# Attention and feed-forward on one core: two queues for the first q and k, gain products on GpSimd, w_in in one go, sums of the last heads in pieces

## The chip, the cores and the metric

The kernel runs on 1 core of one Trainium2 chip. The time is device microseconds of one launch. The kernel before took 425.52 us, the median of three runs (425.33 to 425.61). Inside the core five engines work from instruction queues of their own and meet at semaphores: TensorE (PE, whose weight loads stand apart as PEld), VectorE (DVE), ScalarE (ACT), GpSimd (POOL) and SyncE (SP). SP, ACT and POOL can issue DMAs. In the profile, queue q1 is what SP issues, q0 is what POOL issues, and q10 is what ACT issues.

## The reference, cut to what matters

Eight batches of twelve heads with 448 positions and 64 values a head. Rows of q and k are normalised to unit root mean square and multiplied by gains; attention follows, and its result goes through a feed-forward layer of 768 to 2048 to 768 with a tanh GELU.

```python
def rmsnorm(x, g):
    rms = np.sqrt(np.mean(x * x, axis=-1, keepdims=True) + 1e-06)
    return x / rms * g
q_n, k_n = (rmsnorm(q, g_q), rmsnorm(k, g_k))
scores = np.matmul(q_n, k_n.transpose(0, 1, 3, 2)) / np.sqrt(64)
scores = scores - np.max(scores, axis=-1, keepdims=True)
attn = np.exp(scores)
attn = attn / (np.sum(attn, axis=-1, keepdims=True) + 1e-09)
x = np.matmul(attn, v)            # -> (tokens, 768), heads side by side
h = x @ w_in
g = 0.5 * h * (1.0 + np.tanh(c * (h + 0.044715 * h * h * h)))
out = g @ w_out
```

## The kernel before

**Tiles.** A batch b has three chunks c of four heads. A chunk's q or k is one tile `raw` of 128 x 2 x 7 x 64 floats: two heads by 64 rows on the partitions, two pairs of heads a, and seven tiles t of positions. `square` squares it, `total` sums the squares on DVE (L139), `rsqrt` makes the inverse root on ACT with a logarithm and an exponential (L163 to L173), `normed` multiplies (L210), `turn` transposes on PE (L228) and `put` copies from PSUM to `qT` or, with the product of the two gains as a factor, to `kT` (L237 to L241). The gains come by two small DMAs to `grow`; `gprod` is their product, `gcols` its transpose, `gdiag` a diagonal matrix of it, and the matmul `gall` with `gdiag` yields the bound `shift` that the exponential takes in place of the row's maximum.

**Units.** `unit(b, c, t)` has four score matmuls `sc` (L270) and one exponential `ex` of 128 x 896 on ACT (L274). There are two score buffers in PSUM, so the scores of a unit wait for the exponential two units earlier. `products(b, c, 0)` adds the exponentials up over the keys with a matrix of ones, 28 matmuls; `products(b, c, 1)` multiplies them with v, 28 more (both L315). Both write the PSUM pair `oall`, so the second has to wait until `turned` (two 32 x 32 transposes on DVE, L324) has read the sums. `recips` makes reciprocals in every row (L330, L331), `quad_x` multiplies and writes `xT` (L339).

**Order.** The order is written out by hand. `first_attention` walks the 21 units of batch 0 and calls, after unit i, the functions that the table `mid` holds for slot i, and before it those of `side` (loads of batch 1). `idle(n, warm())` issues n matmuls of zeros that only keep PE busy. After the last unit come the sums and products of chunk 2 and the first two pairs of the first feed-forward matmul (`mm1_pair`, L412: two columns of 128 of w_in, "early" for the inputs of chunks 0 and 1, "late" for those of chunk 2, then the GELU at L417). Six more pairs follow, beside them the norms of batch 1, whose middle chunk is transposed by DMA (`dma_trans`, L251). Then `attention(1, ...)` runs the units of batch 1 two at a time with the second feed-forward matmul of batch 0 between them (`mm2`, L368): 96 matmuls, first all that use the left half of w_out, from the 49th on those that use the right half (`order.sort`, L429).

**Queues.** SP issues q and k of every chunk and the transposes, in program order. POOL issues the gains, v, w_in as two halves of four DMAs each (`w_in_part`, L544) and w_out as two halves (`w_out_part`, L547), all in its own order of work, between squares and norms. A tile of raw q or k has four buffers, so the load of a chunk waits for the norm of the chunk four before it; one buffer (`held`) is kept back until `released`.

**The front before** is these lines: ACT squares the halves of q, then of k, and each norm's root is made as soon as its two sums are there; DVE makes the gain products between the sums of k.

```python
    for n, ns in (("q", q_only), ("k", k_only)):
        for a in range(2):
            square(0, 0, n, nc.scalar, slice(a, a + 1))
            ...
            total(0, 0, n, slice(a, a + 1))
        rsqrt(0, 0, ns, (1,) if n == "k" else ())
    normed(0, 0, "q", nc.gpsimd)
    square(0, 1, "q", nc.gpsimd)
    square(0, 1, "k", nc.gpsimd)
    load_v(0, 0, HP)
```

Of the kernel before, what the change touches and what calls it, by code (L numbers as in the profile page):

```python
# [17 lines left out]
def kernel(  # L18
# [50 lines left out]
    zeros = consts.tile([128, S], BF16)  # L69
    nc.vector.memset(zeros, 0.0)  # L70
# [4 lines left out]
    for i, row in enumerate((g_q, g_k)):  # L75
        nc.gpsimd.dma_start(
            grow[:, i].rearrange("(j p) d -> j p d", j=2)[:, 0],
            row.rearrange("(j d) -> j d", j=2),
        )
# [20 lines left out]
    def load(b, c, n, parts=1, eng=nc.sync):  # L100
        t = rawqk.tile([P, 2, NT, D], F32, tag=f"raw{n}", name=f"raw{n}")
        src = {"q": q, "k": k}[n]
        raws[n, b, c] = t
        m = 2 // parts
        return [
            lambda i=i: eng.dma_start(
                t[:, i * m:(i + 1) * m].rearrange("p a t d -> p a (t d)"),
                src[b, 4 * c + 2 * i * m:4 * c + 2 * (i + 1) * m].rearrange(
                    "(a r) (p t) d -> (r p) a (t d)", r=2, t=NT
                ),  # L110
            )
            for i in range(parts)
        ]
# [86 lines left out]
    def idle(n, w):  # L200

        for _ in range(n):
            nc.tensor.matmul(w, zeros[:, :128], zeros, start=True, stop=True)
# [94 lines left out]
    def products(b, c, what, part=0, parts=1):  # L298

        if part == 0:  # L300
            oas[what] = [o[:, :S] for o in oall]
            if b == 0 and c + 1 == NCH and not what:
                oas[what] = [
                    ps_m.tile([128, 512], F32, tag="mm", name="os")[:, :S] for r in range(2)
                ]
        o = oas[what]
        es = [exs[b, c][:, t] for t in range(NT)]
        if not what and added(b, c):
            es[:added(b, c) + 1] = [ess[b, c]]
        n = len(es)  # L310
        for i in range(n * part // parts, n * (part + 1) // parts):
            for r in range(2):
                rs = slice(r * R, (r + 1) * R)
                for a in range(2):
                    nc.tensor.matmul(  # L315
                        o[r][a * D:(a + 1) * D],
                        vb[b % 2][rs, 2 * c + a, i] if what else ones[rs], es[i][rs, a],
                        start=(i == 0), stop=(i == n - 1),
                    )
# [168 lines left out]
    def first_attention(side, mid):  # L488

        for i in range(NCH * NT):  # L490
            for fn in side.get(i, ()):
                fn()
            unit(0, i // NT, i % NT)
            for fn in mid.get(i, ()):
                fn()
        nc.scalar.preload_act_table_set(GELU_SET)
        square(1, 2, "q", nc.scalar)
        square(1, 2, "k", nc.scalar)
        c = NCH - 1
        products(0, c, 0, 1, 2)  # L500
        turned()
        products(0, c, 1)
        recips()
        mm1_pair(0, early)
        quad_x(0, c)
        mm1_pair(1, early)
        mm1_pair(0, late)
        mm1_pair(1, late)
# [7 lines left out]
    for n in "qk":  # L516
        for go in load(0, 0, n, 2):
            go()
# [48 lines left out]
    for n, ns in (("q", q_only), ("k", k_only)):  # L567
        for a in range(2):
            square(0, 0, n, nc.scalar, slice(a, a + 1))
            if (n, a) == ("k", 1):  # L570
                for h in range(2):
                    nc.vector.tensor_mul(gprod[h * D:(h + 1) * D], grow[:, 0], grow[:, 1])
                nc.vector.transpose(gcols, gprod)
                nc.vector.tensor_scalar(gdiag, ident[:D, :D], gcol[:D], None, op0=ALU.mult)
            total(0, 0, n, slice(a, a + 1))
        rsqrt(0, 0, ns, (1,) if n == "k" else ())
    normed(0, 0, "q", nc.gpsimd)
# [5 lines left out]
    w_in_part(0, 2)  # L583
    gall = ps_s.tile([128, 2, 512], F32, tag="sc", name="gall")[:, 0, :D]
    nc.tensor.matmul(gall, rows, gdiag, start=True, stop=True)
    idle(3, warm())
    turn(0, 0, "q")
    put(0, 0, "q", eng=nc.scalar)
    normed(0, 0, "k", nc.vector, t_first)
    turn(0, 0, "k", t_first)  # L590
# [3 lines left out]
    nc.vector.tensor_scalar(shift, shift, 60.0, 0.0, op0=ALU.add, op1=ALU.min)  # L594
    put(0, 0, "k", t_first)
    idle(3, warm())
# [3 lines left out]
    def released():  # L600
        for t in held:
# [17 lines left out]
            lambda: products(0, 0, 0, 0, 2)),  # L619
           (8, lambda: products(0, 0, 0, 1, 2), lambda: turned(), lambda: recips(),  # L620
            lambda: rsqrt(0, 2, near=(1,)), lambda: normed(0, 2, "q", nc.gpsimd),
            lambda: normed(0, 2, "k", nc.vector, t_first),
            lambda: w_in_part(1, 2),
# [5 lines left out]
           (10, lambda: products(0, 0, 1, 0, 2)),  # L629
           (11, lambda: products(0, 0, 1, 1, 2)),  # L630
# [3 lines left out]
           (15, lambda: products(0, 1, 0, 0, 2), lambda: total(1, 0, "q"),  # L634
            lambda: total(1, 0, "k")),
           (16, lambda: products(0, 1, 0, 1, 2), lambda: turned(), lambda: recips()),
           (18, lambda: products(0, 1, 1, 0, 2)),
           (19, lambda: products(0, 1, 1, 1, 2), lambda: quad_x(0, 1)),
           (20, lambda: products(0, 2, 0, 0, 2))]
# [107 lines left out]
```

## Time and profile before

| | |
|---|---|
| median of three runs | 425.52 us (425.33 to 425.61) |
| the profiled execution's own time | 423.37 us |
| its span | 421.6 us, so 1.77 us lie outside the span |
| PE busy | 405.7 us (96%) |
| ACT busy | 274.9 us (65%) |
| DVE busy | 259.8 us (62%) |
| POOL busy | 124.3 us (29%) |
| first scores / first exponential / last exponential of batch 0 ends | 11.10 / 11.54 / 35.48 us |
| first matmul of the feed-forward layer | 37.28 us |
| first scores of batch 1 | 57.58 us |

All times below are from the start of the span. A line of the timeline gives start, duration, engine, line, operation, out<-in, how many, and in brackets how long the engine had been idle and what ended that. The chain that ended last is followed back from the last instruction, each step to what released it. A row of the windows holds the busy time of PE, PEld, DVE, ACT and POOL in that stretch, each with the number of instructions in brackets, then the granted PE clock as a share, the mean busy share of the DMA engines, and GB/s. A queue's row in the DMA view holds packets, MB and the share of the DMA engines.

### The profile page before, as it was taken

How to read it: one execution, taken by the hardware profiler on the slowest of the kernel's cores; microseconds unless marked ns; L12 is line 12 of the kernel's file. 1: busy time of each engine (PE TensorE's matmuls, PEld its weight loads, DVE VectorE, ACT ScalarE, POOL GpSimd, SP SyncE). 2: the span in 40 equal slices, each digit the busy share in tenths (PEclk: the TensorE clock that was granted, in tenths of full speed). 3: DMA queues.
4: the chain of work that ended last, by engine and by line, in shares of the span. 5: the costliest groups of instructions: out<-in, count | busy, mean ns of one | idle time of the engine just before them, and what ended most of it. 6: DMA issues, size and time to landing. Idle time of an engine off the chain costs nothing.

```text
span 421.6 us, 8029 instructions
## 1 busy us (share of the span) xinstructions
PE 405.7 (96%) x3321; PEld 205.7 (49%) x3321; DVE 259.8 (62%) x430; ACT 274.9 (65%) x364; POOL 124.3 (29%) x98
## 2 busy tenths in 40 slices
PE   5879999999999999999999999999999999999995
PEld 2336554545444544455444554445445454445563
DVE  4887947945689357973689455992589504891010
ACT  5885468838876587838877478747878348754300
POOL 5793515292202640063301840054400900000000
PEclk9998999999999999999999999999999999999999
DMA  7999999589521946249511958239411621130033
GB/s 261 208 256 243 218 192 280 96 205 264 78 62 41 241 79 181 76 104 294 98 39 39 215 129 191 64 83 268 64 46 39 125 45 38 39 75 3 0 75 76
DMA packets 65316, 54.06 MB, mean 128 GB/s; under 512 B 37376, under 2 KB 60288, under 8 KB 65280
## 3 DMA queue, kind: packets, MB, share of 16 engines
q1 hardware_dynamic: 52992, 41.66, 38.0%
q0 software_dynamic: 12128, 11.80, 17.7%
q8 instruction: 26, 0.43, 0.4%
q10 hardware_dynamic: 160, 0.10, 0.1%
q14 instruction: 10, 0.08, 0.1%
HBM read 45.61 MB, written 11.01 MB: 134 GB/s over the span
## 4 chain that ended last, share of the span: by engine, by line
PE 86%; ACT 9%; DVE 2%; POOL 2%; issue 1%; DMA 1%; DVEq 0%; ACTq 0%; POOLq 0%
PE o L368 32%; PE h L348 23%; PE hh L412 12%; PE o L315 9%; PE sc L270 8%; ACT ex L274 5%; ACT L710 2%; DVE ss L139 1%; POOL sq L134 1%; PE tp L228 1%; ACT g L354 1%; DMA rawq<-in_q_dram 1%; POOL win L544 1%; PE os L315 0%; DVE nrmk L210 0%
## 5 line engine op out<-in xcount | busy, mean ns | idle before, releaser
L274 ACT ACTIVATE ex<-sc,shift 128x896 bf16<-128x896 f32 x168 | 159.2, 1004 | 33.3 <-PE sc L270 31.9
L368 PE MATMUL o<-wout,g 128*128 128x384 bf16 x896 | 159.3, 327 | 0.0
L368 PEld LDWEIGHTS <-g 128*128 128x128 bf16 x896 | 81.3, 98 | 71.3 <-issue 23.3
L348 PE MATMUL h<-xT,win 128*128 128x448 bf16 x504 | 96.5, 352 | 0.0
L139 DVE TENSOR_REDUCE ss<-sq 128x14 f32<-128x896 f32 (+1 forms) x43 | 44.4, 1039 | 55.6 <-ACT sq L132 51.6
L348 PEld LDWEIGHTS <-win 128*128 128x128 bf16 x504 | 49.3, 98 | 46.0
L354 ACT ACTIVATE g<-h 128x448 bf16<-128x448 f32 x84 | 45.6, 543 | 28.2 <-PE h L348 23.1
L391 DVE COPY osb<-o 128x384 f32<-128x384 f32 x51 | 28.0, 550 | 58.3 <-PE o L368 58.0
L270 PE MATMUL sc<-qT,kT 64*64 64x448 bf16 x672 | 53.7, 366 | 4.7 <-ACT ex L274 3.5
L417 ACT ACTIVATE g<-hh 128x896 bf16<-128x896 f32 x22 | 19.3, 915 | 57.1 <-PE hh L412 57.1
L412 PE MATMUL hh<-xT,win 128*128 128x448 bf16 x264 | 52.9, 353 | 0.3 <-ACT g L417 0.3
L557 POOL COPY mark<-es 1x1 bf16<-1x1 bf16 x6 | 1.1, 177 | 139.7 <-DVE es L292 139.7
L210 POOL TENSOR_TENSOR nrmq<-rawq,rinv 128x896 bf16<-128x896 f32 x21 | 35.5, 1689 | 17.8 <-DVE o L195 11.9
L315 PE MATMUL o<-ex,vb 64*64 64x448 bf16 x672 | 38.1, 357 | 1.4 <-DVE st L324 1.4
L412 PEld LDWEIGHTS <-win 128*128 128x128 bf16 x264 | 24.6, 98 | 26.1 <-issue 5.0
L270 PEld LDWEIGHTS <-kT 64*64 64x64 bf16 x672 | 17.5, 104 | 37.1 <-issue 33.8
L210 POOL TENSOR_TENSOR nrmk<-rawk,rinv 128x896 bf16<-128x896 f32 x19 | 31.9, 1679 | 0.0
L324 DVE STREAM_TRANSPOSE st<-o 128x448 f32<-128x448 f32 x46 | 27.0, 625 | 6.8 <-PE o L315 6.7
L339 DVE TENSOR_TENSOR xT<-o,rb 128x448 bf16<-128x448 f32 x48 | 27.6, 618 | 4.7 <-PE o L315 4.2
L134 POOL TENSOR_TENSOR sq<-rawq 128x896 f32<-128x896 f32 x9 | 15.6, 1733 | 50.5 <-DVE ss L139 37.8
L315 PEld LDWEIGHTS <-vb 64*64 64x64 bf16 x672 | 20.4, 108 | 15.1 <-issue 4.6
L295 DVE TENSOR_TENSOR e<-ex 128x896 bf16<-128x896 bf16 x38 | 23.2, 611 | 7.0 <-ACT ex L274 7.0
(77 smaller groups left out, 266.0 us busy)
## 6 DMA issues: line engine op xcount, KB each, us to landing
out_dram<-osb SPq DMA_DIRECT2D x54, 192.0 KB, 2.7
rawq<-in_q_dram SPq DMA_DIRECT2D x23, 448.0 KB, 4.4
rawk<-in_k_dram SPq DMA_DIRECT2D x23, 448.0 KB, 4.9
vb<-in_v_dram POOLq DMA_DIRECT2D x8, 672.0 KB, 6.7
win<-in_moe_w_in_dram POOLq DMA_DIRECT2D x8, 384.0 KB, 13.7
wout<-in_moe_w_out_dram POOLq DMA_DIRECT2D x2, 1536.0 KB, 29.4
rawq<-in_q_dram SPq DMA_DIRECT2D x2, 224.0 KB, 2.6
rawk<-in_k_dram SPq DMA_DIRECT2D x2, 224.0 KB, 4.2
```

The lines of the kernel that those rows point to most:

```text
L139: nc.vector.reduce_sum(sss[b][:, c, "qk".index(n), hs], sqs[n, b, c][:, hs], axis=AX.X)
L210: eng.tensor_mul(nrms[n, b, c][:, ts].rearrange("p t a d -> p a t d"), raws[n, b, c][:, :, ts], root[:, :, ts].to_broadcast([P, 2, m, D]),)
L270: nc.tensor.matmul(sc[r * R:(r + 1) * R, a, :S], kT[rs, c, t, r], qT[b][rs, c, :, r], start=True, stop=True,)
L274: nc.scalar.activation(ex[:, t], sc[:, :, :S], AF.Exp, scale=scale, bias=shift)
L315: nc.tensor.matmul(o[r][a * D:(a + 1) * D], vb[b % 2][rs, 2 * c + a, i] if what else ones[rs], es[i][rs, a], start=(i == 0), stop=(i == n ...
L324: nc.vector.transpose(st[:, r].rearrange("p a b -> p (a b)"), oas[0][r])
L339: nc.vector.tensor_mul(xT[b][:, 2 * c + r], oall[r][:, :S], oas["rb"][:, r])
L348: nc.tensor.matmul(h[:, :S], win[:, c, f * 128:(f + 1) * 128], xT[b][:, c], start=(c == 0), stop=(c == HP - 1),)
L354: nc.scalar.activation(g[:, f, (b % 2) * S:(b % 2 + 1) * S], h[:, :S], AF.Gelu_apprx_tanh)
L368: nc.tensor.matmul(o[:, :HD], g[:, f, i * 128:(i + 1) * 128], wout[:, f, half * HD:(half + 1) * HD], start=(f == 0), stop=(f == nf - 1),)
L391: nc.vector.tensor_copy(part, o[:, :HD])
L412: nc.tensor.matmul(h[:, j, :S], win[:, c, f * 128:(f + 1) * 128], xT[b][:, c], start=(c == 0), stop=(c == HP - 1),)
```

## The change

Six things change, all of them in what is issued before the end of batch 0's attention.

The first q and k still come as two halves each, but the first half of both is issued by SP and the second half of both by ACT. ACT issues the second half of q, the two gains and the second half of k, in this order, and only then loads its table of exponentials; before, SP issued all four halves and POOL the gains. The clearing of `grow` comes ahead of that of `zeros`.

The two products of the gains and the scaling of the identity move from DVE to GpSimd; their transpose stays on DVE and stands between the sums of q and those of k.

The root of q is made after the squares of k, not ahead of them, with that of k behind it. GpSimd norms q in two parts, four tiles and three tiles of positions; PE turns and ACT copies them in these parts too, with the first part of k turned between them. The bound `shift` is made ahead of k's norm, and one warming matmul fewer is issued.

The second half of w_in is issued right behind the first, ahead of the norm of q of chunk 2. Before it was issued behind that norm.

The sums of squares of batch 1's first chunk are taken later by DVE: q's at slot 14, k's at slot 16 and behind `turned` and `recips` of chunk 1; before, both came ahead of them.

The sums of chunk 2 get their own PSUM pair (`spared`) at slot 17 and are made in pieces: three of the seven key tiles at slot 17, three behind the products of chunk 1 at slot 20, one after the last unit. Before, three were made at slot 20 and four after the last unit. The products of chunk 1 are cut in three pieces over slots 18, 19 and 20 where they were two, at 18 and 19.

```diff
-    zeros = consts.tile([128, S], BF16)
-    nc.vector.memset(zeros, 0.0)
...
-    for i, row in enumerate((g_q, g_k)):
-        nc.gpsimd.dma_start(
+    zeros = consts.tile([128, S], BF16)
+    nc.vector.memset(zeros, 0.0)
+    def load_gains():
+        for i, row in enumerate((g_q, g_k)):
+            nc.scalar.dma_start(
...
-    def products(b, c, what, part=0, parts=1):
-        if part == 0:
-            oas[what] = [o[:, :S] for o in oall]
-            if b == 0 and c + 1 == NCH and not what:
-                oas[what] = [
-                    ps_m.tile([128, 512], F32, tag="mm", name="os")[:, :S] for r in range(2)
-                ]
+    spare = []
+    def spared():
+        spare.append(
+            [ps_m.tile([128, 512], F32, tag="mm", name="os")[:, :S] for r in range(2)]
+        )
+    def products(b, c, what, lo=0, hi=NT):
+        if lo == 0:
+            oas[what] = spare.pop() if spare else [o[:, :S] for o in oall]
...
-        for i in range(n * part // parts, n * (part + 1) // parts):
+        for i in range(lo, min(hi, n)):
...
-        products(0, c, 0, 1, 2)
+        products(0, c, 0, 6)
...
-    for n in "qk":
-        for go in load(0, 0, n, 2):
-            go()
+    halves = [go for pair in zip(load(0, 0, "q", 2, (nc.sync, nc.scalar)),
+                                 load(0, 0, "k", 2, (nc.sync, nc.scalar))) for go in pair]
+    halves[0]()
+    halves[2]()
+    load_gains()
+    halves[1]()
+    halves[3]()
     nc.scalar.preload_act_table_set(EXP_SET)
...
     idle(16, warm())
-    for n, ns in (("q", q_only), ("k", k_only)):
+    for h in range(2):
+        nc.gpsimd.tensor_mul(gprod[h * D:(h + 1) * D], grow[:, 0], grow[:, 1])
+    for n in "qk":
         for a in range(2):
             square(0, 0, n, nc.scalar, slice(a, a + 1))
-            if (n, a) == ("k", 1):
-                for h in range(2):
-                    nc.vector.tensor_mul(gprod[h * D:(h + 1) * D], grow[:, 0], grow[:, 1])
-                nc.vector.transpose(gcols, gprod)
-                nc.vector.tensor_scalar(gdiag, ident[:D, :D], gcol[:D], None, op0=ALU.mult)
             total(0, 0, n, slice(a, a + 1))
-        rsqrt(0, 0, ns, (1,) if n == "k" else ())
-    normed(0, 0, "q", nc.gpsimd)
+        if n == "q":
+            nc.vector.transpose(gcols, gprod)
+    nc.gpsimd.tensor_scalar(gdiag, ident[:D, :D], gcol[:D], None, op0=ALU.mult)
+    rsqrt(0, 0, q_only)
+    rsqrt(0, 0, k_only, (1,))
+    normed(0, 0, "q", nc.gpsimd, t_first)
+    normed(0, 0, "q", nc.gpsimd, t_rest)
     square(0, 1, "q", nc.gpsimd)
     square(0, 1, "k", nc.gpsimd)
     load_v(0, 0, HP)
     square(0, 2, "q", nc.gpsimd)
     square(0, 2, "k", nc.gpsimd)
     w_in_part(0, 2)
+    w_in_part(1, 2)
...
-    turn(0, 0, "q")
-    put(0, 0, "q", eng=nc.scalar)
-    normed(0, 0, "k", nc.vector, t_first)
-    turn(0, 0, "k", t_first)
+    turn(0, 0, "q", t_first)
+    put(0, 0, "q", t_first, nc.scalar)
     nc.vector.tensor_reduce(
         shift, gall, axis=AX.X, op=ALU.max, apply_absolute_value=True, negate=True
     )
     nc.vector.tensor_scalar(shift, shift, 60.0, 0.0, op0=ALU.add, op1=ALU.min)
+    normed(0, 0, "k", nc.vector, t_first)
+    turn(0, 0, "k", t_first)
+    turn(0, 0, "q", t_rest)
+    put(0, 0, "q", t_rest, nc.scalar)
     put(0, 0, "k", t_first)
-    idle(3, warm())
+    idle(2, warm())
...
              lambda: normed(0, 2, "k", nc.vector, t_first),
-            lambda: w_in_part(1, 2),
             lambda: square(1, 0, "q", nc.gpsimd), lambda: square(1, 0, "k", nc.gpsimd),
...
-           (15, lambda: products(0, 1, 0, 0, 2), lambda: total(1, 0, "q"),
+           (14, lambda: total(1, 0, "q")),
+           (15, lambda: products(0, 1, 0, 0, 3)),
+           (16, lambda: products(0, 1, 0, 3), lambda: turned(), lambda: recips(),
             lambda: total(1, 0, "k")),
-           (16, lambda: products(0, 1, 0, 1, 2), lambda: turned(), lambda: recips()),
+           (17, lambda: spared(), lambda: products(0, 2, 0, 0, 3)),
            (18, lambda: products(0, 1, 1, 0, 2)),
-           (19, lambda: products(0, 1, 1, 1, 2), lambda: quad_x(0, 1)),
-           (20, lambda: products(0, 2, 0, 0, 2))]
+           (19, lambda: products(0, 1, 1, 2, 4)),
+           (20, lambda: products(0, 1, 1, 4), lambda: quad_x(0, 1),
+            lambda: products(0, 2, 0, 3, 6))]
```

## The prediction

> **What bounds the kernel now.** I read the page first (PE busy 96%), then the chain that ended last for the first 75 us, the timeline of the same stretch, the clock by windows, and the DMA queues stretch by stretch.
>
> The front, by the timeline:
>
> ```profile
> 3.31 1.11 ACT L132 ACTIVATE sq<-rawq 128x448 f32<-128x448 f32 x2 [1.28 <-DMA rawq<-in_q_dram]
> 5.75 1.68 POOL L210 TENSOR_TENSOR nrmq<-rawq,rinv 128x896 bf16<-128x896 f32 x1 [2.96 <-ACT rinv L173]
> 6.79 0.58 ACT L132 ACTIVATE sq<-rawk 128x448 f32<-128x448 f32 x1 [0.66 <-DMA rawk<-in_k_dram]
> 8.38 1.68 POOL L134 TENSOR_TENSOR g<-rawq 128x896 f32<-128x896 f32 x1 [0.95 <-DMA rawq<-in_q_dram]
> 11.10 0.38 PE L270 MATMUL sc<-qT,kT 64*64 64x448 bf16 x4
> ```
>
> k's second half lands at 6.79 and sets the first scores at 11.10. The middle, by the chain:
>
> ```profile
> 22.99 2.53 POOL win L544 x4
> 25.54 3.34 POOL sq L134 x2
> 28.90 1.08 DVE ss L139
> 29.98 1.10 DVE st L324 x2
> ```
>
> GpSimd issues half of w_in, so its squares are late, DVE waits for them, and PE for DVE's transposes. ACT then idles 1.94 us at 32.60 and 0.86 us at 34.47. By windows, the stretch with the stall is followed by one at half clock:
>
> ```profile
> 28.03:31.44 3.41, 1.50 (x26) 0.63 (x21) 2.82 (x5) 2.64 (x3) 3.41 (x4) 1.00 1.11 263
> 31.44:34.85 3.41, 3.41 (x44) 2.25 (x39) 2.22 (x3) 1.39 (x2) 3.41 (x3) 0.50 1.11 249
> ```
>
> So far the change aims well. The next place is decisive. The chain around 69 us, the timeline there and later, and the DMA view from 34 us on:
>
> ```profile
> 68.35 1.41 PE o L368 x8
> 69.75 0.04 issue
> 69.79 0.32 PE o L368
> ```
>
> ```profile
> 68.28 1.84 PE L368 MATMUL o<-wout,g 128*128 128x384 bf16 x9
> 78.30 1.64 PE L368 MATMUL o<-wout,g 128*128 128x384 bf16 x9
> ```
>
> ```profile
> wout<-in_moe_w_out_dram POOLq DMA_DIRECT2D x1, 1536.0 KB, 35.6
> ```
>
> The right half of w_out is issued at 34.12 and lands 35.6 us later, at 69.75; the first matmul that reads it (the 49th, last of those nine) starts at 69.79. Nine such matmuls take 1.64 us elsewhere and 1.84 here: PE waits 0.2 us already. What comes earlier than this place gains nothing unless this landing comes earlier. The queues, for 45 to 53, 53 to 63 and 63 to 70 us:
>
> ```profile
> q0 software_dynamic: 2046, 1.64, 129.8%
> q1 hardware_dynamic: 1, 0.00, 0.0%
> ```
>
> ```profile
> q0 software_dynamic: 1860, 1.43, 90.9%
> q1 hardware_dynamic: 1836, 0.47, 36.6%
> ```
>
> ```profile
> q1 hardware_dynamic: 1255, 2.08, 93.0%
> q0 software_dynamic: 200, 0.15, 14.2%
> ```
>
> q0 (w_out, v) runs alone, 0.205 MB/us, then beside SP's transposes at 0.143, and only its last 0.15 MB meet the raw q and k of batch 2.
>
> **The change part by part.**
>
> *Two queues, and roots later.* ACT issues four DMAs: 0.41 us each by SP's rows, 0.60 by ACT's own at the end (two in 1.20). Its table load (1.28) then ends at 3.9 to 4.4 instead of 2.03, say 4.2; four squares of 0.56 make 6.45. When k's second half lands is not shown: at best 5.5 (the four halves' 0.92 MB have passed by 5.3, by the windows' GB/s, and the first landing lagged its bytes by 0.65, less what the gains cost), at worst 6.79 as now. q's root (0.31 + 0.22) thus comes at 7.0 to 7.95, against 5.67. I take 7.2: the bytes bind more than the issue. GpSimd's first part is 4/7 of 1.68, 0.96; the second 0.72. The first scores then come at 9.8 to 10.65, 1.3 to 0.45 us earlier. SP's loads for chunk 1 are issued 0.9 us earlier (two issues fewer) and meet k's second half, which is why I don't take 5.5. One warming matmul fewer (0.2) and the order of two clears cost nothing: PE waits there. Gain products on GpSimd have no row; 0.1 (its memsets) to 0.57 us each (DVE's) fit into the 2.96 us that it idles before 5.75, and they take 1.0 us (0.77 + 0.23) off DVE. If the gains landed late, DVE's transpose would hold k's sums; before, the second landed 4.6 us after its issue at 2.22, but behind 0.56 to 0.74 us of GpSimd issue.
>
> *GpSimd behind it.* Its first square moves from 8.38 to 8.7 or 9.65, and with it the sum for chunk 1 and the root at 14.22: of the front's gain 1.0 to 0.0 us is left. The second half of w_in (2.53 us) goes into the 2.95 us that GpSimd idled from 18.41; it ends at 20.94 plus 0.3 to 1.3, and q's norm of chunk 2 behind it started at 21.35. So chunk 2's scores come 0.5 us earlier at best and 0.4 later at worst; I take 0.4 earlier. w_in itself lands no sooner: q0 is never empty, in the same order.
>
> *The stall.* GpSimd's squares for batch 1 come 2.5 us earlier, and DVE's two sums (1.08 each) stand behind what PE waits for: DVE's waits of 0.55 twice go, PE's 1.29 and 0.15 too, and ACT's 1.94 and 0.86. Twelve of the sixteen last sums (57 ns each, 0.7 us) move ahead of the last exponential; their cover is PE's wait for DVE at slot 17, and if it is gone they cost 0.7 there. Exponentials back to back (0.92) from 25.17 end at 32.5 instead of 35.48. DVE has the products of chunk 1 to scale first (1.16), so the feed-forward starts at 34.45 instead of 37.35: 2.9 us. With the front, batch 0's attention is 3.3 us shorter (2.5 to 3.4).
>
> *What is late next.* The second half of w_in lands at 42.9 and is needed by the fifth pair, at 46.9 less 3.3: 43.6, just in time (batch 2's first loads, issued 2.4 us earlier behind GpSimd's release, can hold it up by up to 1 us). The right half of w_out is not: PE is there at 66.3 and stands until it lands. And it lands later. The transposes of batch 1 wait for GpSimd's norms (47.37), these for DVE's roots, and these for the end of chunk 2, so SP issues them 3.3 us earlier, and the raw loads of batch 2 behind them. q0 loses 3.3 us of running alone and has 3.3 x 0.205 = 0.68 MB more left when the raw loads begin (59.7 instead of 63). Beside raw loads it moved 0.38 MB in the 4 us from 39 to 43, 0.095 MB/us. So 0.68 MB take 7.1 us, to 66.8, and the 0.15 MB of before, which took 6.75 us, end at 73.5. That is the upper bound; SP's last raw load lands at 73.95 and then q0 would be alone. The lower bound spreads all 0.83 MB evenly over the engines: 59.7 + 8.7 = 68.4. I take 72.0, nearer the upper, because the uneven tail is in the trace. PE resumes 2.2 us later than before.
>
> The DMA view of those 4 us, where both queues had work:
>
> ```profile
> q0 software_dynamic: 419, 0.38, 57.4%
> q1 hardware_dynamic: 419, 0.72, 55.9%
> ```
>
> As many packets of the one as of the other. By the Trainium skill (DMA: Bandwidth & Descriptors, "Queues, rings and completion order") an engine alternates between the queues that have work, packet by packet. The trace agrees, and by this rule the sum is the one above. If instead q0's older work were served first, the landing would stay at 69.75; that is the first rival below.
>
> *The clock.* A stretch of 3.41 us with PE busy 1.50 was followed by 3.41 us at 0.50, which cost 1.7 us of PE work; a standstill of 3 to 7 us does the same, and PE works without a pause behind it. Between 0 and 2.4 us are lost, by where the stretch falls; I take 1.2. The Trainium skill (TensorE: Matmul & The Clock Gate, "Part 1: The HAM clock gate") states a free-running window of 3413 ns; the trace's two stretches fit, and by it the loss is the same but its phase is not the kernel's to choose.
>
> *Sum.* 2.2 + 1.2 = 3.4 us slower: 426.8 for the profiled execution's 423.37. That one ran 2.15 us under the median of the runs; against the median, 425.5 + 3.4 = 428.9. The ends: 1.4 faster with no clock loss, 424.1; 3.7 + 1.7 slower, 430.9. Least of all this depends on the front.
>
> **The rivals.**
>
> *The landing stays at 69.75* because q0's work is served first. The gain is waited away, the clock costs 0 to 1.7: 425.3 to 427.2. The packets of 39 to 43 us speak against it. Chance 0.18, half of it within 0.2%.
>
> *Faster: the uneven tail of q0 goes away.* Without the 6.75 us in which a few engines finish 0.15 MB, w_out lands early. For 0.2% it has to land by 68.9 and PE to keep its clock; landing at 66.4 gives the whole 3.4, 422.1. For it: the first v landed without such a tail, so something between 18 and 24 us makes it, and the order there changes. Likeliest time 423.3. Chance 0.20.
>
> *The front fails.* k's second half lands at 6.79, GpSimd is 1.3 us late, w_in's second half holds up chunk 2 by 0.4. The attention is 2.5 us shorter, q0 starts later by up to 1.3 us, the landing is at 71.2 to 72.5: 427.5 to 429. Chance 0.12.
>
> *My forecast* has 0.50, and 427 to 430.9 as its own range. Slower by over 0.2% (0.85 us, about what measurement can tell from no change): 0.50 + 0.12 + 0.09 = 0.71; within: 0.09; faster: 0.20. The range reaches into the faster case, to 423.8, and to 431.
>
> **What would show it.** Right: the feed-forward starts near 34.0; the first transpose by DMA is issued near 45.8; the 49th matmul of L368 ends an idle time of PE of over 3 us, released by w_out's landing after 70.5; a window at 0.50 behind it and none around 32. For the front: q's table load on ACT ends near 4.2, k's squares begin before 6.8, first scores by 10.2. Wrong: w_out landing before 69, or PE not waiting there; or a start of the feed-forward later than 36, which would leave too little shift for the rest to follow.

## The result, and the profile after

The changed kernel takes 431.63 us (median; 427.60 to 432.22). Its ratio to the kernel before is 1.0132, 95% interval 1.0095 to 1.0170: slower by 1.3%. The forecast was 428.9 with a range of 423.8 to 431.0, so the direction held and the size did not: the medians differ by 6.1 us where 3.4 was forecast. The profiled execution took 431.12 us with a span of 429.3 us, 7.7 us more than before.

The timeline of the front of the changed kernel (start, duration, engine; the lines answer to those of before, with new line numbers):

```profile
1.22 1.08 ACTq L78 DMA_DIRECT2D grow<-in_g_q_dram  x1
2.33 0.50 ACTq L78 DMA_DIRECT2D grow<-in_g_k_dram  x1
2.86 0.41 ACTq L109 DMA_DIRECT2D rawk<-in_k_dram  x1
8.87 0.58 ACT L135 ACTIVATE sq<-rawk 128x448 f32<-128x448 f32 x1 [2.77 <-DMA rawk<-in_k_dram]
10.03 1.83 POOL L213 TENSOR_TENSOR nrmq<-rawq,rinv 128x512 bf16<-128x512 f32 x2 [2.67 <-DMA rawk<-in_k_dram]
11.82 1.68 POOL L137 TENSOR_TENSOR g<-rawq 128x896 f32<-128x896 f32 x1
13.35 0.59 PE L273 MATMUL sc<-qT,kT 64*64 64x448 bf16 x4
15.08 1.04 POOL L125 DMA_DIRECT2D vb<-in_v_dram  x1
```

The second half of k, issued by ACT behind the gains, lands at 8.85 where it landed at 6.77. GpSimd starts the norm of q at 10.03 instead of 5.75, the first scores come at 13.35 instead of 11.10, and v, the first load in q0, is issued at 15.08 instead of 11.64. The front has lost 2.25 us at the scores and 3.44 us at q0. The wait of 2.67 us before the norm stands against a DMA of k, but it ends with q's root: the root is ready at 9.89, and in the same front with w_out in rows, further below, the norm starts at 10.04 behind the root (ACT rinv).

The chain of the changed kernel around the feed-forward layer:

```profile
35.31 40.26 DMA wout<-in_moe_w_out_dram
75.58 0.04 issue
75.62 0.48 PE o L374
```

The right half of w_out is issued 1.2 us later than before, takes 40.26 us instead of 35.6, and is now 9% of the chain. What PE lost to it stands in the page's group of the second feed-forward matmuls (busy us and mean ns, then idle time and what ended most of it; before, that idle time was 0.0):

```profile
L374 PE MATMUL o<-wout,g 128*128 128x384 bf16 x896 | 159.7, 328 | 4.9 <-DMA wout<-in_moe_w_out_dram 4.9
```

PE resumes at 75.62 instead of 69.79, 5.83 us later. The rest, about 1.9 us, lies in the clock, by the windows of the changed kernel:

```profile
8.33:11.74 3.41, 0.61 (x8) 0.45 (x8) 1.59 (x4) 1.66 (x6) 1.71 (x2) 1.00 0.46 177
11.74:18.57 6.83, 6.46 (x33) 1.91 (x32) 3.44 (x5) 4.33 (x8) 6.81 (x6) 0.50 0.66 156
69.77:73.18 3.41, 0.95 (x6) 0.47 (x5) 3.34 (x6) 0.46 (x1) 2.52 (x3) 1.00 1.12 337
73.18:80.01 6.83, 4.39 (x39) 1.58 (x38) 0.66 (x2) 1.91 (x2) 1.67 (x1) 0.50 0.95 218
```

Twice a stretch with an idle PE is followed by 6.83 us at half clock: once in the front, where PE waits for q and k, and once behind the wait for w_out, where PE was busy 4.39 us at half clock and so got about 2.2 us less done. The first scores of batch 2 come at 113.85 instead of 105.98, 7.9 us later, and nothing is lost from there on.

The granted clock of a whole execution differs from run to run of one kernel (0.983 in three runs of the changed kernel, which took 431.12 to 432.22 us, and 0.992 in the one of 427.60), so a profiled execution can lie several us from its kernel's median. Ratios below leave out the slow runs, those more than 1.5% above the fastest of their kernel: one of the eight of the front alone (431.88 us) and two of the six of one queue with w_out in rows (427.11 and 427.80; with them the means give 0.996 there, with an interval that reaches past 1). Medians are of all runs, and the other numbers are those of one profiled execution.

### The profile page after: what moved, and what is told of

It is laid out like the page before. It is cut to its first block, busy times and chain, and to the rows that moved or that the text cites. A ratio compares the mean times of both kernels' runs of the same rounds, so it can differ in the third digit from the quotient of the medians.

```text
span 429.3 us, 8029 instructions
## 1 busy us (share of the span) xinstructions
PE 409.4 (95%) x3320; PEld 205.1 (48%) x3320; DVE 258.7 (60%) x427; ACT 275.0 (64%) x365; POOL 124.1 (29%) x100
## 4 chain that ended last, share of the span: by engine, by line
PE 76%; DMA 11%; POOL 5%; ACT 5%; issue 1%; SPq 0%; DVE 0%; ACTq 0%; POOLq 0%
PE o L374 30%; PE h L354 22%; DMA wout<-in_moe_w_out_dram 9%; PE o L321 8%; PE hh L418 8%; PE sc L273 7%; ACT ex L277 3%; POOL g L137 2%; ACT L727 2%; DMA rawk<-in_k_dram 1%; POOL win L554 1%; POOL sq L137 1%; DMA rawq<-in_q_dram 1%; ACT g L360 1%; POOL nrmq L213 0%
## 5 line engine op out<-in xcount | busy, mean ns | idle before, releaser
L213 POOL TENSOR_TENSOR nrmq<-rawq,rinv 128x896 bf16<-128x896 f32 (+2 forms) x22 | 35.6, 1622 | 14.4 <-DVE o L198 11.0
L418 PEld LDWEIGHTS <-win 128*128 128x128 bf16 x264 | 24.6, 98 | 26.1 <-issue 5.0
L337 DVE STREAM_TRANSPOSE rb<-rc 128x896 f32<-128x896 f32 x24 | 26.7, 1111 | 0.8
```

Of the source, the lines that this page charges most:

```text
L213: eng.tensor_mul(nrms[n, b, c][:, ts].rearrange("p t a d -> p a t d"), raws[n, b, c][:, :, ts], root[:, :, ts].to_broadcast([P, 2, m, D]),)
L418: nc.tensor.matmul(h[:, j, :S], win[:, c, f * 128:(f + 1) * 128], xT[b][:, c], start=(c == 0), stop=(c == HP - 1),)
```

## The experiments

The numbers of all of them in one place. "q0 to SP" is the time from the issue of v (q0's first large load) to SP's first transpose for batch 1, so how long q0 runs before SP's traffic joins it; "lag" is from that transpose to the landing of the right half of w_out, where it is loaded whole; "wait" is PE's wait for w_out.

| kernel | first scores | feed-forward | q0 to SP | lag | w_out lands | wait | ratio to before |
|---|---|---|---|---|---|---|---|
| before | 11.10 | 37.28 | 37.5 | 20.6 | 69.75 | 0.2 | 1 |
| changed | 13.35 | 38.25 | 34.4 | 26.1 | 75.58 | 4.90 | 1.0132 (1.0095 to 1.0170) |
| middle alone | 11.95 | 35.97 | 35.9 | 23.5 | 71.03 | 2.10 | 0.9995 (0.9962 to 1.0027) |
| front alone | 12.68 | 38.69 | 35.6 | 21.6 | 71.81 | 0.69 | 1.0102 (1.0065 to 1.0139) |
| k ahead of the gains | 12.15 | 36.74 | 33.8 | 26.9 | 74.83 | 5.66 | 1.0103 (1.0072 to 1.0133) |
| early root of q | 12.81 | 37.11 | 34.8 | 23.4 | 71.75 | 2.20 | 1.0051 (1.0027 to 1.0075) |
| one queue | 10.18 | 33.97 | 33.0 | 26.1 | 71.28 | 4.88 | 1.0083 (1.0053 to 1.0112) |
| one queue, 1 raw chunk behind w_out | 10.38 | 34.14 | 33.0 | 25.6 | 70.88 | 4.32 | 1.0054 (1.0032 to 1.0076) |
| one queue, 2 raw chunks behind | 10.23 | 35.92 | 34.1 | 21.6 | 68.75 | 0.40 | 0.9965 (0.9941 to 0.9989) |
| one queue, 3 raw chunks behind | 9.89 | 33.66 | 33.0 | 21.1 | 65.91 | 0 | 0.9920 (0.9889 to 0.9951) |

**The two halves of the change.** The theory after the result: the front loses, by the gains ahead of k in ACT's queue; the middle gains nothing, because w_out then lands later. The middle alone is the kernel before with the new order of products and sums and with w_in in one go:

```diff
+    w_in_part(1, 2)
...
-            lambda: w_in_part(1, 2),
...
+           (14, lambda: total(1, 0, "q")),
+           (17, lambda: spared(), lambda: products(0, 2, 0, 0, 3)),
```

> The kernel before with the middle of the change alone: w_in's second half behind the first, batch 1's sums of squares later, chunk 2's sums in pieces. The front is as before. Theory (the landing of w_out's right half is the bound, and it is late when queue 0 has more left as the raw loads begin): the feed-forward starts near 34.4 instead of 37.28, the first transposes by DMA are issued near 46 instead of 49.1, the right half of w_out lands at 70.5 to 73.5 instead of 69.75, PE waits for it for 3 us or more and works at half clock behind it; time 1 to 5 us over the kernel before. Rival A (the landing does not move): lands at 69.75, time within 1.7 us of before. Rival B (the middle's 2.9 us are kept, and only the front made the change slow): PE does not wait, about 422.5 us.

The feed-forward starts 1.3 us earlier than before, w_out lands 1.3 us later, PE waits 2.10 us, and the time is that of before (424.46 us). The landing moved as the theory said, but the wait is shorter than the 3 us or more that it expected, and its loss of 1 to 5 us did not come: what the middle gained by then, 2.2 us, is waited away, and no more. The front alone is the complement, the changed kernel with the middle of before:

```diff
-    w_in_part(1, 2)
...
-           (17, lambda: spared(), lambda: products(0, 2, 0, 0, 3)),
+           (15, lambda: products(0, 1, 0, 0, 2), lambda: total(1, 0, "q"),
```

> Only what the change does ahead of the first scores (the two queues, the gains on ACT, their products on GpSimd, q's norm in two parts), with the middle of the kernel before and w_in's second half where it was. Theory (the late front is what the change loses by, through GpSimd and q0): first scores near 13.3 and v issued near 15.1 as in the changed kernel; the feed-forward at 40.3 to 41.0; SP's transposes come as much later as q0 does, so the right half of w_out lands at 73 to 74 and PE, itself 3.4 us late, waits 0 to 1 us there; 3.5 to 5 us slower than before, 428.5 to 430.5. Rival (the landing follows from q0's start alone): it lands at 75.6 as in the changed kernel, PE waits 2 us or more, and the time is 431 or more. If the front were harmless, 425 to 426.

Its median is 429.42 us: 1.0% of the 1.3% come with the front. The profiled execution was the quickest of its eight, 425.34 us; in it v is issued at 14.67 and w_out lands at 71.81, earlier than expected, since SP's transposes are later as well and the lag is only 1 us longer. Batch 2's first scores are 2.1 us later than before there: 1.4 us by the later feed-forward and 0.5 by a longer wait for w_out. So in that execution the front loses mostly by being late itself. The slower ones had a lower granted clock (0.983 to 0.992 against 0.994); where their stretches fall, and so what makes up the rest of the 1.0%, is not shown.

**What in the front.** Three runs undo one thing each in the changed kernel. First, k ahead of the gains in ACT's queue:

```diff
-    load_gains()
     halves[1]()
     halves[3]()
+    load_gains()
```

> The changed kernel, but ACT issues k's second half ahead of the two gains (order: q's second half, k's second half, gains). In the changed kernel k's second half is issued at 2.86, its packets begin near 5.0 and it lands at 8.85. Theory (it is late because it is issued behind the gains, whose two issues take 1.6 us, and so meets SP's loads for chunk 1): it lands by 6.5, the root of q comes near 8 instead of 9.9, v is issued near 13 instead of 15.1, the right half of w_out lands 2 us or more earlier than 75.6; time 428 or less. Rival (what lies on ACT's queue is served late whatever the order): it lands at 8 or later, and the time stays at 431.

k's second half lands at 5.45 instead of 8.85, so its place behind the gains was what held it up. But now the gains are late, by the timeline of this run:

```profile
7.73 0.57 POOL L578 TENSOR_TENSOR gprod<-grow 64x32 f32<-64x32 f32 x2 [6.41 <-DMA grow<-in_g_k_dram]
8.33 0.21 DVE L584 STREAM_TRANSPOSE gcols<-gprod 128x32 f32<-128x32 f32 x1 [1.93 <-POOL gprod L578]
8.47 1.11 DVE L142 TENSOR_REDUCE ss<-sq 128x7 f32<-128x448 f32 x2
```

The transpose of the gains stands ahead of k's sums on DVE, so DVE stood 1.93 us. Only 0.96 us reached GpSimd's norm of q (9.07), w_out landed 0.75 us earlier, and PE, which came earlier too, waited longer. The time, 429.85 us, missed the 428 or less that was expected. Second, the root of q as soon as its sums are there:

```diff
         if n == "q":
             nc.vector.transpose(gcols, gprod)
-    nc.gpsimd.tensor_scalar(gdiag, ...)
-    rsqrt(0, 0, q_only)
+            nc.gpsimd.tensor_scalar(gdiag, ...)
+            rsqrt(0, 0, q_only)
```

> The changed kernel, but the root of q (and the scaling of the identity) comes behind the sums of q and ahead of k's squares, as before the change. Theory (the late root makes GpSimd issue v 3.4 us later than before, so queue 0 starts later and the right half of w_out lands later): GpSimd norms q near 7.5 instead of 10.0, v is issued near 12.5 instead of 15.1, the right half of w_out lands near 73 instead of 75.6; the first scores stay at 13.0 to 13.4, since k's second half is as late as before. Time 428 to 429.5. Rival (the landing follows the scores and the transposes, not the start of queue 0): it lands at 75 or later, and the time stays.

v is issued 1.54 us earlier than in the changed kernel, w_out lands 3.83 us earlier, and 4.2 us of the median are gone (427.44 us). GpSimd's norm began at 8.49, not 7.5: the scaling of the identity, which waits for the gains, stands ahead of it. Of the three edits this one gives back most, 0.8 of the 1.3%, although k's second half is still late and the first scores still come at 12.81: what it brings forward is q0. Third, all four halves of q and k by SP, and only the gains by ACT:

```diff
-    halves = ... load(0, 0, "q", 2, (nc.sync, nc.scalar)) ... load(0, 0, "k", 2, (nc.sync, nc.scalar))
+    halves = ... load(0, 0, "q", 2, (nc.sync, nc.sync)) ... load(0, 0, "k", 2, (nc.sync, nc.sync))
```

> The changed kernel, but SP issues all four halves of the first q and k, in the order q, k, q, k, and ACT issues the gains alone. Theory (k's second half is late because it waits on ACT's queue behind the gains): it lands by 6.8, as before the change, the gains near 5, the root of q is made near 8, v is issued near 13, first scores near 11.2; the right half of w_out lands near 73.5; time 427 to 429. Rival (the bytes or the four issues ahead are what makes k late): it lands after 8.

The expectation, and the one of the kernel with one queue and w_out in rows, name the order q, k, q, k; the edit and the trace have both halves of q and then both of k, as before the change. k's second half lands at 5.93, GpSimd's norm starts at 7.11, the first scores come at 10.18 and the feed-forward at 33.97. (Why k lands 0.84 us earlier than in the kernel before, with the same order on the same queue, is not shown.) These are the times that the prediction assumed for its front, and the rest went as it said:

```profile
71.32 0.32 PE L374 MATMUL o<-wout,g 128*128 128x384 bf16 x1 [4.88 <-DMA wout<-in_moe_w_out_dram]
```

The feed-forward starts 3.3 us earlier than before, PE arrives 3.2 us earlier at the 49th matmul and stands 4.88 us; 428.62 us, still 0.8% slower than before.

**Whether the wait is what costs.** If so, a right half of w_out that comes in two pieces lets PE start on the first. The edit in `w_out_part`, the same in six kernels:

```diff
+        for j in range(1 + i):
+            m = nf // (1 + i)
             nc.gpsimd.dma_start(
-                wout[:, :, i * HD:(i + 1) * HD], ...
+                wout[:, j * m:(j + 1) * m, i * HD:(i + 1) * HD], ...
```

In the kernel with the middle alone:

> As the middle alone, and the right half of w_out comes as two DMAs of 1024 rows each instead of one of 2048, so that the 49th matmul waits for the first eight tiles of rows only. Theory: the first DMA lands 5 us or more before the second, PE waits for it little or not, and the second is there before its first use some 3 to 4 us later: the middle's 2.9 us are kept, 421.5 to 424 us, and no stretch at half clock near 70 us. Rival (PE's wait there is not for w_out's bytes, or the second DMA lands too late): time as with the middle alone.

The wait is gone and the ratio is 0.9970 (0.9948 to 0.9993), 424.11 us: a gain of about 1.3 us, where the theory kept 2.9. In the changed kernel:

> The changed kernel with the right half of w_out in two DMAs of rows. The changed kernel's PE waits 4.9 us at 75.6 and works at half clock until 80. Theory: both go for the most part; what is left against before is the front, 1.0 us at the feed-forward's start, less 0.2: 425.5 to 427. Rival (the 2.25 us at the first scores are what the change costs, and the wait only shows it): time stays at 430 or more.

425.57 us, ratio 1.0014 (0.9983 to 1.0044): by the ratios 1.2 of the 1.3% are back, although the late front is still there. A wait of 2.42 us for the second piece at 76.14 is left. In the kernel before, as a control:

> The kernel before with the right half of w_out in two DMAs of rows and nothing else. PE waits 0.2 us there before. Theory: 0 to 0.3 us faster, the same by measurement; it shows that the split pays only where PE comes early. Rival (the split itself is worth the 0.3% that the middle with the split gained): 1.3 us faster.

424.46 us, 0.9984 (0.9964 to 1.0003): the cut itself is worth almost nothing where PE did not wait. With one queue, where PE came earliest:

> The changed kernel with all four halves of the first q and k on SP's queue (q, k, q, k), and with the right half of w_out loaded as two pieces of 128 x 8 rows instead of one. Theory (only the landing of the right half keeps the earlier front and the shorter middle from showing): the feed-forward starts at about 34.0, the first piece lands before PE needs it at 66.4, the second at about 71.3, where PE needs it at about 70.4 (4.0 us behind the 49th matmul, as in the changed kernel with the same cut). So PE waits 0 to 1 us instead of 4.88, and the whole is 4 to 6 us shorter than with one queue alone: 422.5 to 424.5 as a median, faster than the kernel before by 0.2% to 0.7%. Rival 1 (q0's bytes bind, however they are cut): the second piece lands at 74 to 76 and PE waits 3.5 us or more there, 427 to 429. Rival 2 (the wait is not what costs): the wait goes and the time stays at 428.6.

422.21 us, 0.9918 (0.9890 to 0.9946). Four of its six runs, 420.23 to 422.33 us, are faster than both kernels; the two at 427.11 and 427.80 are not. The profile is of the fastest. The pieces land at 61.62 and 70.55, and PE goes through:

```profile
65.23 1.64 PE L374 MATMUL o<-wout,g 128*128 128x384 bf16 x9
68.63 0.50 PE L374 MATMUL o<-wout,g 128*128 128x384 bf16 x2
```

The shorter attention, which one queue alone turned into a loss, is worth 0.66% in those four runs against the control. With q's root early as well:

> As the run before it, and q's root and the scaling of the identity are made directly behind q's squares, ahead of k's. Theory (whatever lets GpSimd start v and the weights earlier brings the landing forward by as much or more): GpSimd's norm of q starts 0.6 to 1.2 us earlier than at 7.11, v is issued at 11.0 to 11.6, the last piece of w_out lands 1 to 2 us earlier, and no wait is left: 421.5 to 423.5. Rival (k's roots then come later on ACT, and first scores with them): first scores 10.2 to 10.8 instead of 10.18, and the time no better than the run before it.

425.48 us, 0.9991 (0.9966 to 1.0017): no gain, a miss. The norm of q did start at 6.41, but the square behind it then stood 1.54 us for raw q of chunk 1, which landed late, so v was issued at 13.06 instead of 12.43, and a wait of 2.55 us for w_out came back. An attempt to keep two queues, with k's half on ACT right behind q's, the gains on POOL, their products on DVE, q's root early, the new middle and w_out in pieces:

> The middle with w_out's right half in two DMAs, and the first halves on two queues, with ACT's second half of k right behind its second half of q; the gains stay on GpSimd, their products on DVE and the root of q ahead of k's squares, as before the change. Theory (two queues help when nothing stands ahead of k, and the late root and the gains' place are what cost): k's second half lands near 5.5 instead of 6.8, first scores at 9.8 to 10.4, v is issued by 11.9, no wait for w_out; 1 us faster than the middle with w_out in rows, 422.5 to 423.5. Rival (the first loads are bound by their bytes): k's second half lands at 6.5 to 6.8, time as with the middle and w_out in rows, 424.

424.65 us, 1.0014 (0.9979 to 1.0049), no gain. k's second half lands at 5.22, but the first scores come at 19.32 in the profiled execution, one of the five of its twelve runs that took 428.59 us or more (the other seven took 422.85 to 424.73); what held DVE there is told under the unexpected things.

**Why w_out lands late.** The prediction said: because the raw loads of batch 2, which SP issues, share the DMA engines with it. SP issues three raw chunks behind its first transposes: the middle and the last of batch 2 and the first of batch 3. From the kernel with one queue, the raw q and k of batch 2's last chunk were moved into q0, behind w_out:

```diff
-                  (5, lambda: loads(2, 2),
-                   lambda: square(2, 0, "q", nc.gpsimd),
+                  (5, lambda: square(2, 0, "q", nc.gpsimd),
                    lambda: square(2, 0, "k", nc.gpsimd),
+                   lambda: loads(2, 2, nc.gpsimd)),
```

> The changed kernel with all four halves of the first q and k on SP's queue, w_out whole, and one thing more: the raw q and k of batch 2's last chunk (0.92 MB) are issued by POOL, behind w_out in q0, instead of by SP beside it. Theory (the right half of w_out lands late because raw loads share the DMA engines with it): between 59.9 us and the landing, q1 moved 2.56 MB and q0 0.74 MB; with 0.92 MB of q1 moved behind w_out, 0.74 + 1.64 MB at 0.289 MB/us take 8.2 us at most, so the landing comes at 66.5 to 68.1 instead of 71.28, PE waits 0.1 to 1.7 us instead of 4.88, and the whole is 3 to 6 us shorter than with one queue alone: 422.5 to 425.5. Rival (q0 moves at a pace of its own there, or its issue time sets the landing): it stays at 70.5 to 71.5, PE waits 4 us or more, 427.5 to 429.5. Second rival (the late chunk is then late for its norm): the wait goes, and DVE or PE waits for the sums of that chunk near 75 to 85 us instead.

The theory's numbers missed: the landing moved by 0.4 us, as the rival said. The DMA view of the kernel with one queue, from 59.9 us to the landing (packets, MB, share), shows why the sum by bytes was the wrong one:

```profile
q1 hardware_dynamic: 1524, 2.56, 66.7%
q0 software_dynamic: 966, 0.74, 42.0%
```

A raw chunk (448 KB of q and of k, in rows of seven tiles by 64 floats) is 512 packets of 1792 bytes. From 63.2 to 68 us, while both queues had work, they moved nearly equal numbers of packets and very unequal numbers of bytes:

```profile
q1 hardware_dynamic: 583, 0.99, 62.6%
q0 software_dynamic: 537, 0.40, 53.7%
```

If the engines take one packet of each queue in turn, w_out's last 966 need about 966 raw packets to be held up in full, and the two chunks left with SP have 1024. So batch 2's middle chunk was moved too, then the first of batch 3:

```diff
-                   lambda: normed_both(1, 2, nc.vector), lambda: loads(2, 1)),
+                   lambda: normed_both(1, 2, nc.vector)),
...
+                   lambda: loads(2, 1, nc.gpsimd), lambda: loads(2, 2, nc.gpsimd)),
...
-                side.append((1, lambda: loads(b + 3, 0)))
+                side.append((1, lambda: loads(b + 3, 0, nc.sync if b else nc.gpsimd)))
```

> As the run before it, and the raw q and k of batch 2's middle chunk go behind w_out into q0 as well. SP keeps one chunk, of 512 packets, beside the rest of w_out. Theory (the engines alternate packet by packet, so what counts is how many raw packets lie ready while w_out's last 966 go): in the run before, two chunks, 1024 packets, were still ready, as many as w_out needs to be held up in full, and so nothing moved. Now 512 are: 0.72 MB of w_out and 0.92 MB of raw data from 60.9 us at 0.29 MB/us end at 66.6 us on the mean engine and at about 68.6 on the last; PE waits 0 to 2.2 us instead of 4.32. Rival 1 (the landing has nothing to do with the raw loads): 70.5 to 71.5 again. Rival 2 (byte share): each chunk taken away would have moved it alike, and the first did so by 0.4 us, so 70.0 to 70.9.

The last line of the edit belongs to the next run alone:

> All three raw chunks that SP issues behind the transposes go into q0 behind w_out; no raw packet lies beside it. Theory: 0.72 MB alone at 0.205 MB/us from 60.9 us land at 63.5 to 65.5, before PE is there at 66.4; no wait at the 49th matmul, no stretch at half clock behind it. What can take its place: the middle chunk's raw data then land at 67 to 70 instead of 63 to 68, and GpSimd's squares and DVE's sums behind them later too. 422 to 425, against 427.3 to 428.6 with the wait. Rival 1 (the landing has nothing to do with the raw loads): 70.5 to 71.5 and a wait of over 4 us again. Rival 2 (the later raw data stop DVE and with it PE): no wait at w_out, but one of PE for DVE's copies between 70 and 90, 426 or more.

The timelines at the 49th matmul, with one chunk moved:

```profile
70.92 0.48 PE L374 MATMUL o<-wout,g 128*128 128x384 bf16 x1 [4.32 <-DMA wout<-in_moe_w_out_dram]
```

with two:

```profile
68.80 0.32 PE L374 MATMUL o<-wout,g 128*128 128x384 bf16 x1 [0.40 <-DMA wout<-in_moe_w_out_dram]
```

and with all three (the 49th is the last of the nine), its only long wait in this stretch a new one for DVE:

```profile
64.66 1.64 PE L374 MATMUL o<-wout,g 128*128 128x384 bf16 x9
78.42 0.38 PE L321 MATMUL o<-ex,vb 64*64 64x448 bf16 x2 [1.81 <-DVE st L330]
```

Without raw packets beside it w_out lands at 65.91, 5.4 us earlier, PE does not wait for it, and the time is 422.18 us, ratio 0.9920 (0.9889 to 0.9951), faster than both kernels in all six runs. The landing is 0.4 us later than the theory's latest. So the cause of the late landing is shown for the kernel with one queue; the changed kernel has the same lag, 26.1 us, but was not run with these edits. By dose the lag is 26.1, 25.6, 21.6 and 21.1 us with 3, 2, 1 and 0 chunks beside w_out. A share by bytes does not give this order: the first chunk taken away did nearly nothing. The packet rule asked for some 23 us with one chunk, by its later bound; in that execution q0 had run 1.1 us longer ahead of SP, which may be the difference. The Trainium skill (DMA: Bandwidth & Descriptors, "Queues, rings and completion order") states that a DMA engine goes round the queues it has work for, one packet at a time; its packet is a bundle of descriptors and need not be the one that the profile counts. The nearly equal counts above and the first two doses agree with it.

## Why the prediction was right or wrong

**The bound** was named rightly. The landing of w_out's right half decides: cutting the load gives 1.2% back in the changed kernel, although a wait of 2.42 us is left there, and in the kernel before, where PE waited 0.2 us, it gives 0.16%, with an interval that includes no change.

**The landing term** was right in kind and in size, if it is counted from SP's first transpose. The forecast put that transpose at 45.8 and the landing at 72.0, a lag of 26.2 us; measured were 26.14 us in the changed kernel and 26.12 with one queue, against 20.62 before. The closeness is in part luck: 72.0 was picked out of 68.4 to 73.5. The table shows the lag growing as q0's time ahead of SP shrinks, though not strictly (front alone and middle alone). That shrinking has two sources that the prediction had as one: SP coming earlier (one queue: transposes 3.97 us earlier, v 0.53 later) and q0 starting later (changed kernel: transposes 0.31 us later, v 3.44 later). In the changed kernel q0 so ran ahead for 34.4 us, close to the 34.2 with which the forecast worked (37.5 less 3.3), but because q0 started late and not because SP came early. The rival in which q0's older work is served first is excluded by the last three runs. For the one in which q0's uneven tail goes away nothing spoke: with w_out whole and SP's loads as they were, it never landed before 69.75.

**The step that failed is the front**, in "Two queues, and roots later": k's second half "at best 5.5, at worst 6.79 as now". It landed at 8.85. The upper bound was taken from a load that stood in SP's queue; in the new place it stands behind two small DMAs of ACT's and beside SP's loads of chunk 1. That SP's loads meet it was said, and used only to move the value inside the bounds. The issue of the gains was mis-sized too: 1.08 and 0.50 us where 0.41 to 0.60 each were taken, so ACT's table load ended at 4.58 instead of 4.2. The DMA view of the changed kernel from 4.5 to 5.0 us, where q10 has no row:

```profile
q1 hardware_dynamic: 97, 0.17, 97.7%
```

From 4.0 to 5.0 us ACT's queue moved 4 packets and SP's, already at chunk 1, 203. That the place behind the gains is what held k up is shown by the run with k ahead of them, where k is issued 1.65 us earlier and lands 3.40 us earlier (5.45). Why it took until 8.85 beside SP's loads is not shown in more detail. The steps behind inherit it: q's root 9.89 instead of 7.2, first scores 13.35 instead of 9.8 to 10.65, GpSimd's first square 11.82 instead of 8.7 to 9.65, q0 3.44 us late. The prediction's own sign for this was a feed-forward later than 36; it came at 38.25 instead of 34.0.

The prediction also read the front of the kernel before wrongly where it says that k's second half "sets the first scores". The chain of that kernel does not pass through this load. Its square was done at 7.37, but DVE was at the gain products until 8.19 and took k's last sum only then:

```profile
6.16 0.62 DVE ss L139
6.91 0.57 DVE gprod L572
8.19 0.61 DVE ss L139
```

So 0.8 us of the gain that one queue shows at the first scores can come from taking these products off DVE, whatever k's landing does.

**The sum.** PE resumed at 75.62 where the forecast had 72.0; these 3.6 us are the 3.64 us by which SP's first transpose was later than forecast (49.44 against 45.8). The clock cost 1.9 us (7.7 less 5.83) where 1.2 of 0 to 2.4 was taken. Together 3.4 + 3.6 + 0.7 = 7.7 for the profiled pair. The upper end of the range took only 1.7 for the clock; with the 2.4 of its own paragraph it would have been 431.6. "Least of all this depends on the front" was the false sentence: a late front moves q0, and with it every landing behind it. The rival "the front fails" had the right sign, but was bounded by the same 6.79.

**The stall** gained 2.2 us with the middle alone and 2.4 with one queue, by the time from first scores to feed-forward (26.2 before, 24.0, 23.8), where 2.9 was forecast; in the changed kernel 1.3, with 6.83 us of it at half clock. GpSimd's gain products did fit into its idle time (5.99 to 7.36), and the last load of w_in, at 46.29 instead of 42.89, kept nobody waiting.

With a front at the times that it assumed (one queue), the forecast of 428.9 us was met by a median of 428.62, from runs of 426.41 to 432.01.

## What to carry to other kernels

A load that moves to another queue has none of its old bounds: its landing is set by what stands ahead of it there, however small, and by what the other queues have ready in the meantime (8.85 us here behind two gains, 5.45 ahead of them). When the next thing that ends last is a long load, ask for each edit how it moves the start of that load's queue and the start of the traffic beside it; work that comes earlier can also bring forward the traffic that holds the load up. Such a load can be freed by cutting it where its first reader can start, or by putting the competing loads behind it in its own queue; here the second turned a loss of 0.8% into a gain of 0.8% in all six runs, the first in four of six.

## What was not expected of the hardware

Tiny DVE instructions took up to 17 times as long (3.85 us instead of 0.23) when GpSimd worked beside them. The scaling of the identity took 0.23 us before, in a gap of GpSimd's; in the kernel before with w_out in two pieces it fell beside a square:

```profile
7.83 1.68 POOL L134 TENSOR_TENSOR g<-rawq 128x896 f32<-128x896 f32 x1 [0.23 <-DMA rawq<-in_q_dram]
8.21 1.33 DVE L577 TENSOR_SCALAR gdiag<-ident,gcols 64x64 bf16<-64x64 bf16 x1
```

and with two queues and the gains apart, where the products and the scaling each met two of GpSimd's instructions:

```profile
8.04 1.67 POOL L134 TENSOR_TENSOR g<-rawq 128x896 f32<-128x896 f32 x1
8.35 3.04 DVE L578 TENSOR_TENSOR gprod<-grow 64x32 f32<-64x32 f32 x2 [0.93 <-DMA grow<-in_g_k_dram]
9.68 1.67 POOL L134 TENSOR_TENSOR g<-rawk 128x896 f32<-128x896 f32 x1
11.75 3.85 DVE L580 TENSOR_SCALAR gdiag<-ident,gcols 64x64 bf16<-64x64 bf16 x1
```

Each ends when an instruction of GpSimd beside it ends (9.51, 11.35, and for the last a square from 13.88 to 15.56). The Trainium skill (SBUF — State Buffer, "Who interferes with whom") says that DVE and GpSimd share a pair of ports, that a `tensor_scalar` in a two-port mode or a `tensor_tensor` with both inputs in SBUF can contend for it, and that whoever issues first keeps it for a whole instruction while the other stands. The first two cases agree, with GpSimd issuing first; the last began at 11.75, while GpSimd was only issuing v's DMA, so there the order is not shown. In the kernel before with w_out in two pieces the scaling takes 1.10 us longer and k's norm starts 1.28 us later (10.66 instead of 9.38). The first scores come 2.16 us later (13.26 instead of 11.10); PE's granted clock is 0.50 there from 9.6 to 13.3 us, and 1.00 in the kernel before from 9.6 to 11.2. With the gains apart they come at 19.32. That the medians differ for it is not shown. Moving these products to GpSimd, as the change does, takes them out of that contest.
